# Weight tiles loaded by casting DMAs from GpSimd instead of f32 loads and casts on two engines

## The chip, the cores and the metric

The kernel runs on one core of a Trainium2 chip. The metric is the device time of one execution in microseconds, as the median of several runs. The engines are named as in the profile: PE is TensorE (PEld its weight loads), DVE is VectorE, ACT is ScalarE, POOL is GpSimd, SP is SyncE, which here only issues DMAs. A name with a q behind it (SPq, POOLq) is the queue of that engine.

## The reference, cut to what matters

The program is an attention with two branches, followed by a two-layer dense block.

```python
# batch 8, heads 8, seq 576, head_dim 64; q, k, v float32
q_d, k_d, v_d = means of q, k, v over groups of 4 tokens          # 144 tokens
out_up    = repeat(softmax(q_d @ k_d.T / 8) @ v_d, 4)             # pooled branch
scores    = where(|i - j| < 4, q @ k.T / 8, -1e9)                 # local branch
out_local = softmax(scores) @ v
x = (out_up + out_local) as [4608 tokens, 512]
h = x @ w_in                  # w_in  [512, 2048]
g = h - tanh(h)
out = g @ w_out               # w_out [2048, 512], out [4608, 512] float32
```

## The kernel before, in words

**Attention.** Heads are taken two at a time: 32 head pairs, four to a batch, numbered p = 0 to 31. For each pair, q and k are loaded as f32 into `qkn` (4 buffers), cast and reordered into `qr` (L416), transposed on TensorE (L442) and copied into `qk` (L448). Pairs are pooled over four tokens by two additions (L459, L464). v is loaded in windows of 120 tokens into `vst` (5 buffers) and cast into `vw` (L351, the step `prep_v`). Local scores go to `ps_ts` (L478), exponentials to `E` (L511, L521, L524), a mask is multiplied in (L514, L527), and the products with v go to `ps_ox` (L538, L545). They are normalized into `ln` (L554, L556), transposed back (L566 to L570), and added with the pooled part into `xT` (L597, L599), which holds x transposed in bf16. Pairs 0 to 3 use two sets of PSUM banks in turn; later pairs use one set, since the other becomes the banks `ps_hy` of the dense part. From pair 16 on, the two transposes are DMAs.

**Dense part.** The tokens are taken in 9 blocks of 512. `mm1` (L619) makes 128 of the 2048 hidden columns of a block with four matmuls, ScalarE takes the tanh (L627) and VectorE the difference into `gT` (L630); `mm2` (L646) sums 16 matmuls per 128 tokens, ScalarE copies the result (L657) and SyncE stores it (L660). A block needs all four pairs of its batches. Weights lie in SBUF in bf16, as `w_in_sb` and `w_out_sb`.

**Weights.** `load_w` loads each weight matrix in four tiles f = 0 to 3 of 1 MB (f32), 512 columns of w_in or 512 rows of w_out each. The f32 tile lands in a staging area that is not used otherwise at that time: halves of the two `gT` buffers, or parts of `xT` that belong to batches 4 to 7. Four casts for each tile (L344), each 128 x 512, bring it to bf16 in its place. The DMAs are issued from SyncE (L328, L335, L337): the four tiles of w_in behind the loads of pairs 0 to 3, the tiles of w_out one after another between the loads of pairs 4 to 8 (`ORDER`, `load_next`).

**Order.** The kernel notes every step with an engine, an assumed duration, its reads and writes and a priority (`Program.op`); `choice` names several engines for one step, the casts of weights among them. A planner (`Program.order`) then simulates the engines, with all transfers served one by one, and writes each engine's instructions in the order that it found. The order of each engine is therefore fixed when the program is built. A smaller number is a better priority: dense matmuls have 5000, the steps of pair p have 10 p, the reordering casts 10 p - 12, casts of v 10 p - 12, loads -30. Before the first dense matmul, warm-up matmuls on unused data (L802) are put into the holes of TensorE that the plan shows.

Of the kernel before, what the change touches and what calls it, by code (L numbers as in the profile page):

```python
# [8 lines left out]
FP32 = mybir.dt.float32  # L9
# [6 lines left out]
class Program:  # L16
# [18 lines left out]
    def op(self, eng, ns, fn, reads=(), writes=(), pri=0):  # L35
        i = len(self.ops)
        deps = set()
        for key in reads:
            if key in self.last_write:
                deps.add(self.last_write[key])  # L40
        for key in writes:
            if key in self.last_write:
                deps.add(self.last_write[key])
            deps.update(self.readers.get(key, ()))
        for key in reads:
            self.readers.setdefault(key, set()).add(i)
# [104 lines left out]
def kernel(  # L151
# [9 lines left out]
    nc = tc.nc  # L161
# [3 lines left out]
    NP = H // 2  # L165
# [23 lines left out]
    NQKN, NVST, NVW = 4, 5, 3  # L189
# [25 lines left out]
    gT = fixed("gT", [128, N_FF, 512], BF16, 2)  # L215
# [18 lines left out]
    P = Program()  # L234
    op = P.op
    V, A, T, GP = nc.vector, nc.scalar, nc.tensor, nc.gpsimd
# [45 lines left out]
    def load(ns, fn, keys, cost, pri):  # L282
        op("SP", ns, fn, writes=list(keys) + ["queue", ("q", keys[0])], pri=pri)
        op("DMA", cost, None, reads=[("q", keys[0])], writes=keys, pri=pri)
# [36 lines left out]
                op("DVE", 100, clear, writes=[("vst", s, i)], pri=-99)  # L321
            load(1000, issue, [("vst", s, i)], T_V, -30)

    def load_w(src, dst, name, f, stage, keys):

        def issue():
            if src is moe_w_in:
                nc.sync.dma_start(out=stage.rearrange("p (c f) -> p c f", c=4),  # L328
                                  in_=src[:, 512 * f:512 * f + 512].rearrange(
                                      "(c p) f -> p c f", p=128))  # L330
            else:
                rows = src.rearrange("(f p) n -> p f n", p=128)
                if isinstance(stage, list):
                    for c in range(4):
                        nc.sync.dma_start(out=stage[c], in_=rows[:, 4 * f + c, :])  # L335
                else:
                    nc.sync.dma_start(  # L337
                        out=stage.rearrange("p (c f) -> p c f", c=4),
                        in_=rows[:, 4 * f:4 * f + 4, :])
        load(600, issue, keys, T_W, -30)  # L340
        for c in range(4):
            part = stage[c] if isinstance(stage, list) else stage[:, 512 * c:512 * c + 512]
            to = dst[:, c, 512 * f:512 * f + 512] if src is moe_w_in else dst[:, 4 * f + c, :]
            P.choice([(eng, ns, lambda part=part, to=to, fn=fn: fn(out=to, in_=part))  # L344
                      for eng, ns, fn in CAST], reads=keys, writes=[(name, f, c)],
                     pri=W_PRI + f)


    def prep_v(p):
        s, w, jj = p % NVST, (p // 2) % NVW, p % 2  # L350
        P.choice([(eng, ns, lambda fn=fn: fn(  # L351
            out=vw[w][:, 2 * jj:2 * jj + 2, :, 0:64], in_=vst[s]))
                  for eng, ns, fn in CAST_V[p >= NEARLY]],
                 reads=[("vst", s, 0), ("vst", s, 1)],
                 writes=[("vw", w, jj)], pri=10 * p - 12)
# [327 lines left out]


    M2_FIRST, T_DMA, X_DMA, NEW = 16, 16, 16, 16
    ORDER = "p0p1p2p3"
    T_QK, T_V, T_W, W_PRI, NEARLY = 1150, 900, 2850, -3, NP
    CAST = [("POOL", 700, GP.tensor_copy), ("ACT", 520, A.copy)]
    CAST_V = [[("POOL", 720, GP.tensor_copy), ("ACT", 640, A.copy)],
              [("POOL", 720, GP.tensor_copy)]]  # L690
    any3 = [("DVE", 600, V.tensor_copy), ("ACT", 740, A.copy),
# [9 lines left out]
    for i in range(2):  # L701
        def guards(i=i):
# [3 lines left out]
           writes=[("qk", i, a) for a in range(2)])  # L706
    for i in range(NVW):
        def ones(i=i):
# [3 lines left out]
           writes=[("vd", i), ("vw", i, 0), ("vw", i, 1)])  # L712
        op("POOL", 200, lambda i=i: GP.affine_select(
            out=vd[i][:, 1, :, 64], in_=vd[i][:, 1, :, 64], compare_op=ALU.is_ge,
            fill=0.0, base=-112, pattern=[[0, 4]], channel_multiplier=1),
           writes=[("vd", i)], pri=-96)
    for i in range(2):
        op("DVE", 70, lambda i=i: V.memset(E[i][:, 1728:1840], 0.0),
           writes=[("E", i, 2)], pri=-94)
# [3 lines left out]
    for p in range(NP):  # L723
        if p + 1 < NP:
            load_qk(p + 1)
        load_v(p)
    stages = []
    for g in range(2):
        t = gT[g].rearrange("p f c -> p (f c)").bitcast(FP32)
        for e in range(2):  # L730
            stages.append((t[:, 2048 * e:2048 * e + 2048],
                           [("gT", g, 8 * e + c) for c in range(8)]))
    for e in range(2):
        stages.append(([xT[c][:, 2304 + 1024 * e:3328 + 1024 * e].bitcast(FP32)
                        for c in range(4)],
                       [("x", 4 + 2 * e, c) for c in range(4)]))
    for f in range(4):
        load_w(moe_w_in, w_in_sb, "w_in", f, *stages[f])
    queue = list(ORDER)
    nl = [NP]  # L740

    def load_next():

        while queue and queue[0] != "p":
            f = int(queue.pop(0))
            load_w(moe_w_out, w_out_sb, "w_out", f, *stages[(4, 5, 2, 3)[f]])
        if queue:
            queue.pop(0)
        if nl[0] < NPAIR:
            load_qk(nl[0])  # L750
            load_v(nl[0])
            nl[0] += 1
        if not queue or "p" not in queue:
            while queue:
                f = int(queue.pop(0))
                load_w(moe_w_out, w_out_sb, "w_out", f, *stages[(4, 5, 2, 3)[f]])

    for p in range(2):
        prep_v(p)
    made = 0  # L760
    for i in range(2):
        op("DVE", 70, lambda i=i: V.memset(qkd[i][:, 288:344], 0.0),
           writes=[("qkd", i)], pri=-94)
        op("DVE", 70, lambda i=i: V.memset(vp[i][:, :, :, 64:65], 4.0),
           writes=[("vp", i)], pri=-94)
# [4 lines left out]
    for p in range(NPAIR):  # L770
        if p % 2 == 0 and p < NEW:
            pool_v(p // 2)
        if p + 2 < NPAIR:
            prep_v(p + 2)
        if p == 0:
            next(work[1])
        next(work[p])
        if p + 1 >= NP and p + 1 < NPAIR:
            next(work[p + 1])
        next(work[p], None)  # L780
        if p + 2 < NP:
            next(work[p + 2])
        load_next()
        if NEW <= p + 1 < NPAIR:
            pool_v4(p + 1)
        if NEW <= p + 3 < NPAIR:
            load_v4(p + 3)
        if p % NP == NP - 1:
            b = p // NP
            while made < NBLK and ((made + 1) * 512 - 1) // S <= b:  # L790
                dense(made)
                made += 1
# [41 lines left out]
```

## Time and profile before

| | us |
|---|---|
| median of three runs | 348.71 (348.31 to 348.74) |
| span of the profiled execution | 346.3 |
| the profiled execution's own time | not listed; the span stands for it |
| first dense matmul (L619) starts | 32.06 |
| last instruction of ACT ends | 342.8 |

A row of instructions gives the start in us, the duration in us, the engine, the line, the operation, the tile written and read, the shape, and in brackets the idle time of the engine just before it with what ended it. [...] A group row has the count behind x, then the busy time in all, the mean ns of one, and the idle time before them. An issue row gives the size and the median us from issue to landing.

### The profile page before, as it was taken

The numbers are of one execution on the slowest core, as the hardware profiler recorded it, in microseconds if no ns is written. First come the engines' busy times: TensorE is split into PE (matmuls) and PEld (weight loads), VectorE is DVE, ScalarE is ACT, GpSimd is POOL, SyncE is SP. The second block draws the span as 40 slices with busy tenths as digits, with TensorE's granted clock in tenths as the row PEclk, the third lists the DMA queues.
The fourth block names the chain that finished last, engine by engine and source line by source line (L and its number), as shares of the span: only waits on it lengthen the run. The fifth ranks groups of instructions, "written<-read, shape, count | busy, mean of one in ns | idle before, by whom it ended". The sixth has DMA issues, their size and how long they took to land.

```text
span 346.3 us, 6847 instructions
## 1 busy us (share of the span) xinstructions
PE 328.0 (95%) x2556; PEld 163.5 (47%) x2556; DVE 223.8 (65%) x362; ACT 224.8 (65%) x382; POOL 169.9 (49%) x210
## 2 busy tenths in 40 slices
PE   6787989999999999999999999899999999999995
PEld 2353445555555554445444444444454444444442
DVE  5675788558897968778867677679774443343300
ACT  4585886768978768787878778599753434343411
POOL 6553555575467856887777786958500000000000
PEclk9698999999999999999999999999999999999999
DMA  8999999999999998999999999645231000100021
GB/s 192 234 374 300 277 262 263 217 216 287 212 222 234 252 234 174 226 231 235 261 221 207 260 233 246 157 92 93 57 85 60 31 32 30 61 32 31 30 93 61
DMA packets 103407, 60.74 MB, mean 175 GB/s; under 512 B 77774, under 2 KB 94670, under 8 KB 103374
## 3 DMA queue, kind: packets, MB, share of 16 engines
q1 hardware_dynamic: 103374, 60.30, 78.5%
q8 instruction: 20, 0.33, 0.4%
q14 instruction: 13, 0.11, 0.1%
HBM read 42.46 MB, written 9.44 MB: 150 GB/s over the span
## 4 chain that ended last, share of the span: by engine, by line
PE 69%; DVE 10%; ACT 9%; issue 3%; DMA 3%; POOL 2%; SPq 1%; ACTq 0%; POOLq 0%; DVEq 0%
PE ps_hy_540 L646 8%; PE ps_hy_538 L619 8%; PE ps_hy_539 L619 7%; PE ps_hy_541 L646 7%; PE ps_hy_538 L646 7%; PE ps_hy_539 L646 6%; PE ps_hy_540 L619 6%; PE ps_hy_541 L619 6%; PE ps_ox L538 3%; DVE qr_87 L416 2%; PE ps_ts L478 2%; DMA qkn_73<-in_k_dram 2%; PE ps_ox L545 2%; PE ps_ts L442 2%; PE ps_ox L389 2%
## 5 line engine op out<-in xcount | busy, mean ns | idle before, releaser
L619 PEld LDWEIGHTS <-w_in_sb 128*128 128x128 bf16 x576 | 53.3, 98 | 62.1 <-issue 3.9
L646 PEld LDWEIGHTS <-gT_110 128*128 128x128 bf16 x320 | 30.2, 98 | 34.5
L646 PEld LDWEIGHTS <-gT_111 128*128 128x128 bf16 x256 | 24.0, 98 | 27.4
L459 POOL TENSOR_TENSOR half<-qk_88 128x576 f32<-128x576 bf16 x14 | 16.4, 1169 | 25.3 <-ACT qk_88 L448 11.2
L459 POOL TENSOR_TENSOR half<-qk_89 128x576 f32<-128x576 bf16 x16 | 18.7, 1167 | 19.8 <-ACT qk_89 L448 12.2
L646 PE MATMUL ps_hy_539<-w_out_sb,gT_110 128*128 128x512 bf16 x80 | 20.7, 379 | 0.0
L646 PE MATMUL ps_hy_540<-w_out_sb,gT_110 128*128 128x512 bf16 x80 | 20.4, 379 | 0.0
L646 PE MATMUL ps_hy_538<-w_out_sb,gT_110 128*128 128x512 bf16 x80 | 20.4, 379 | 0.0
L646 PE MATMUL ps_hy_541<-w_out_sb,gT_110 128*128 128x512 bf16 x80 | 20.1, 379 | 0.0
L432 ACT COPY qk_89<-qT_91 128x576 bf16<-128x576 bf16 x16 | 18.7, 1193 | 0.0
L432 ACT COPY qk_88<-qT_90 128x576 bf16<-128x576 bf16 x16 | 18.4, 1188 | 0.0
L511 ACT ACTIVATE E_100<-ps_ts 128x960 bf16<-128x960 f32 x16 | 15.6, 977 | 3.8 <-PE ps_ts L478 3.8
L556 DVE TENSOR_TENSOR ln_106<-ps_ox,r_104 128x896 bf16<-128x896 f32 x16 | 17.4, 1090 | 0.5
L646 PE MATMUL ps_hy_540<-w_out_sb,gT_111 128*128 128x512 bf16 x64 | 16.9, 379 | 0.0
L646 PE MATMUL ps_hy_541<-w_out_sb,gT_111 128*128 128x512 bf16 x64 | 16.8, 379 | 0.0
L646 PE MATMUL ps_hy_539<-w_out_sb,gT_111 128*128 128x512 bf16 x64 | 16.6, 379 | 0.0
L646 PE MATMUL ps_hy_538<-w_out_sb,gT_111 128*128 128x512 bf16 x64 | 16.4, 379 | 0.0
L511 ACT ACTIVATE E_101<-ps_ts 128x960 bf16<-128x960 f32 x14 | 13.6, 973 | 3.8 <-PE ps_ts L478 3.6
L514 DVE TENSOR_TENSOR E_101<-E_101,mask 128x960 bf16<-128x960 bf16 x16 | 13.1, 820 | 3.9 <-ACT E_101 L511 3.7
L556 DVE TENSOR_TENSOR ln_107<-ps_ox,r_105 128x896 bf16<-128x896 f32 x14 | 15.3, 1090 | 0.4
L514 DVE TENSOR_TENSOR E_100<-E_100,mask 128x960 bf16<-128x960 bf16 x16 | 13.6, 847 | 2.8 <-ACT E_100 L511 2.8
L619 PE MATMUL ps_hy_538<-xT_65,w_in_sb 128*128 128x512 bf16 x36 | 13.9, 385 | 1.2 <-DVE xT_68 L599 1.2
(263 smaller groups left out, 890.1 us busy)
## 6 DMA issues: line engine op xcount, KB each, us to landing
out_dram<-y_115 SPq DMA_DIRECT2D x12, 256.0 KB, 2.6
out_dram<-y_116 SPq DMA_DIRECT2D x12, 256.0 KB, 2.3
out_dram<-y_117 SPq DMA_DIRECT2D x12, 256.0 KB, 3.0
qkn_71<-in_q_dram SPq DMA_DIRECT2D x8, 288.0 KB, 7.8
qkn_71<-in_k_dram SPq DMA_DIRECT2D x8, 288.0 KB, 5.8
qkn_72<-in_q_dram SPq DMA_DIRECT2D x8, 288.0 KB, 5.1
qkn_72<-in_k_dram SPq DMA_DIRECT2D x8, 288.0 KB, 5.5
qkn_73<-in_q_dram SPq DMA_DIRECT2D x8, 288.0 KB, 6.6
```

What stands on the lines that cost most here:

```text
L389: T.matmul(pv[:, 0, :], pick[:, t, :], vw[w][:, :, t, 0:64], start=(t == 0), stop=(t == NT - 1))
L416: P.choice([(eng, ns, lambda dst=dst, srt=srt, fn=fn: fn(out=dst, in_=srt)) for eng, ns, fn in REORDER[p >= NEARLY][i]], reads=[("qkn", sn ...
L432: op("ACT", 600, lambda i=i: A.copy(out=full[:, i].rearrange("p (g a) -> p g a", a=A6), in_=qT[s][:, i].rearrange("p a g -> p g a")), read ...
L442: T.transpose(b16[:, G6 * a:G6 * a + G6], qr[s][:, i, a, :], ident[0:G6, 0:G6])
L459: eng.tensor_tensor(out=half, in0=four[:, :, :, 0:2], in1=four[:, :, :, 2:4], op=ALU.add)
L478: T.matmul(sc[:, c:c + NQ[t]], qk[s][rows, k0:k0 + 128], qk[s][rows, QW * t:QW * t + NQ[t]], start=True, stop=True)
L511: op("ACT", 870, lambda: A.activation(out=e1, in_=ps[:, :, 0:480], func=AF.Exp, scale=SCALE), reads=ts, writes=[("E", s, 0)], pri=pri)
L514: op("DVE", 700, lambda: V.tensor_tensor(out=e1, in0=e1, in1=mask[:, 0:480].unsqueeze(1).to_broadcast([128, 2, 480]), op=ALU.mult), reads= ...
L538: T.matmul(po[:, hh, 65 * t:65 * t + 65], E[s][:, c:c + 128], vw[w][:, 2 * jj + hh, t, :], start=True, stop=True)
L556: op("DVE", 1010, lambda: V.tensor_tensor(out=ln[s].rearrange("p n (h d) -> p h n d", d=D), in0=blocks[:, :, :, 0:64], in1=r[s].unsqueeze( ...
L619: T.matmul(ps_hy[slot], w_in_sb[:, dc, fc * 128:(fc + 1) * 128], xT[dc][:, kb * 512:kb * 512 + 512], start=(dc == 0), stop=(dc == N_DC - 1))
L646: T.matmul(ps_hy[slot], gT[g][:, fc, ts * 128:ts * 128 + 128], w_out_sb[:, fc, :], start=(fc == 0), stop=(fc == N_FF - 1))
```

## The change

`load_w` no longer takes a staging area. One DMA for each tile, issued from GpSimd, reads f32 from memory and writes bf16 straight into `w_in_sb` or `w_out_sb`. The 32 casts, the staging areas and the weight DMAs on SyncE go, and with them `CAST`, `W_PRI` and `ORDER`. Each weight DMA has a gate: it is noted as reading `vw` of a certain pair, so it is issued behind the cast of v of that pair (`W_IN_AT`, `W_OUT_AT`: tiles 0 and 1 of w_in behind pair 2, tiles 2 and 3 of w_in and tile 0 of w_out behind pair 3, the other tiles of w_out behind pairs 4, 5 and 6). The planner counts 1.0 us of GpSimd for an issue, with priority -40, and 2.85 us for the transfer, as before.

```diff
-    def load_w(src, dst, name, f, stage, keys):
-
-        def issue():
...
-        load(600, issue, keys, T_W, -30)
-        for c in range(4):
-            part = stage[c] if isinstance(stage, list) else stage[:, 512 * c:512 * c + 512]
-            to = dst[:, c, 512 * f:512 * f + 512] if src is moe_w_in else dst[:, 4 * f + c, :]
-            P.choice([(eng, ns, lambda part=part, to=to, fn=fn: fn(out=to, in_=part))
-                      for eng, ns, fn in CAST], reads=keys, writes=[(name, f, c)],
-                     pri=W_PRI + f)
-
+    def load_w(src, dst, name, f, gate):
+
+        if src is moe_w_in:
+            to = dst[:, :, 512 * f:512 * f + 512]
+            rows = src[:, 512 * f:512 * f + 512].rearrange("(c p) f -> p c f", p=128)
+        else:
+            to = dst[:, 4 * f:4 * f + 4, :]
+            rows = src.rearrange("(f p) n -> p f n", p=128)[:, 4 * f:4 * f + 4, :]
+        op("POOL", 1000, lambda: nc.gpsimd.dma_start(out=to, in_=rows),
+           reads=[gate], writes=[("wq", name, f)], pri=-40)
+        op("DMA", T_W, None, reads=[("wq", name, f)],
+           writes=[(name, f, c) for c in range(4)], pri=-30)
...
-    ORDER = "p0p1p2p3"
-    T_QK, T_V, T_W, W_PRI, NEARLY = 1150, 900, 2850, -3, NP
-    CAST = [("POOL", 700, GP.tensor_copy), ("ACT", 520, A.copy)]
+    W_IN_AT, W_OUT_AT = (2, 2, 3, 3), (3, 4, 5, 6)
+    T_QK, T_V, T_W, NEARLY = 1150, 900, 2850, NP
...
+    def load_ws(p):
+
+        for f in range(4):
+            if W_IN_AT[f] == p:
+                load_w(moe_w_in, w_in_sb, "w_in", f, ("vw", (p // 2) % NVW, p % 2))
+        for f in range(4):
+            if W_OUT_AT[f] == p:
+                load_w(moe_w_out, w_out_sb, "w_out", f, ("vw", (p // 2) % NVW, p % 2))
 
     for p in range(2):
         prep_v(p)
+        load_ws(p)
...
             prep_v(p + 2)
+            load_ws(p + 2)
```

`load_next` keeps the loads of q, k and v, and loses the ones of w_out.

More of the change, by code (lines that the diff above doesn't have):

```diff
@@ L322, in load_v @@
             load(1000, issue, [("vst", s, i)], T_V, -30)
-    def load_w(src, dst, name, f, stage, keys):
-        def issue():
[L327 to L333, printed above, removed]
-                    for c in range(4):
[L335 to L339, printed above, removed]
-        load(600, issue, keys, T_W, -30)
-        for c in range(4):
-            part = stage[c] if isinstance(stage, list) else stage[:, 512 * c:512 * c + 512]
-            to = dst[:, c, 512 * f:512 * f + 512] if src is moe_w_in else dst[:, 4 * f + c, :]
-            P.choice([(eng, ns, lambda part=part, to=to, fn=fn: fn(out=to, in_=part))
-                      for eng, ns, fn in CAST], reads=keys, writes=[(name, f, c)],
-                     pri=W_PRI + f)
+    def load_w(src, dst, name, f, gate):
[9 more added lines that the diff above has]
+           writes=[(name, f, c) for c in range(4)], pri=-30)
     def prep_v(p):
@@ L726 @@
         load_v(p)
[L727 to L739, printed above, removed]
     nl = [NP]
     def load_next():
[L744 to L748, printed above, removed]
         if nl[0] < NPAIR:
@@ L752, in load_next @@
             nl[0] += 1
[L753 to L756, printed above, removed]
+    def load_ws(p):
[5 more added lines that the diff above has]
+                load_w(moe_w_out, w_out_sb, "w_out", f, ("vw", (p // 2) % NVW, p % 2))
     for p in range(2):
         prep_v(p)
+        load_ws(p)
     made = 0
```

## The prediction

> **What bounds the kernel now.** I read the page first, then the busy time by stretches, then the chain of waits ahead of the first dense matmul, then the instructions in order of time on GpSimd and SyncE. The page:
>
> ```profile
> span 346.3 us, 6847 instructions
> PE 328.0 (95%) x2556; PEld 163.5 (47%) x2556; DVE 223.8 (65%) x362; ACT 224.8 (65%) x382; POOL 169.9 (49%) x210
> DMA  8999999999999998999999999645231000100021
> ```
>
> TensorE is busy 95% of the span, but the transfers are busy too, nine tenths or more in nearly every slice until about 220 us. Which of them sets the end in which stretch is seen in the stretches (columns: length, busy time and instructions of each engine, granted clock, share and GB/s of the transfers). The last row of the fence is the same view for the warm-up matmuls (L802) alone.
>
> ```profile
> 0.00:32.00 32.00, 22.63 (x244) 12.44 (x245) 20.62 (x55) 19.50 (x36) 18.15 (x36) 0.89 1.06 272
> 32.00:45.00 13.00, 12.14 (x68) 5.32 (x68) 8.41 (x12) 8.53 (x16) 6.59 (x9) 0.88 1.12 275
> 45.00:76.00 31.00, 30.77 (x316) 17.21 (x314) 21.21 (x34) 23.02 (x44) 18.47 (x24) 1.00 1.18 243
> 76.00:260.00 184.00, 180.37 (x1553) 91.49 (x1552) 146.03 (x221) 142.75 (x234) 126.71 (x143) 1.00 0.97 201
> 0.00:32.00 32.00, 10.28 (x28) 2.86 (x28) 0.89 1.06 272
> ```
>
> From 45 us on TensorE has no room: idle 0.23 us of 31, then 3.6 us of 184. Before 32 us it is idle for 9.4 us and does warm-up work for 10.3 us, and from 32 to 45 us it loses 0.9 us idle and runs at a mean clock of 0.88. So what this change can win, it wins before 45 us, as an earlier or better filled start; after that only lost TensorE time counts. The chain of waits before the first dense matmul:
>
> ```profile
> 24.07 0.60 ACT vd_84 L396
> 25.82 1.10 DVE ln_106 L556
> 29.00 1.10 DVE ln_107 L556
> 31.24 0.77 DVE xT_68 L599
> ```
>
> It is the chain of head pairs 2 and 3; the last piece of xT (31.24 + 0.77) releases the dense part, not a weight.
>
> **What the casts cost, and where.** The eight 1 MB weight tiles are cast in 32 instructions, half on each engine:
>
> ```profile
> L344 POOL CAST w_in_sb<-gT_110 128x512 bf16<-128x512 f32 x4 | 2.4, 617 | 0.8 <-DMA gT_110<-in_moe_w_in_dram 0.8
> L344 ACT CAST w_in_sb<-gT_110 128x512 bf16<-128x512 f32 x4 | 2.3, 627 | 0.0
> 24.55 1.14 ACT L344 CAST w_in_sb<-gT_110 128x512 bf16<-128x512 f32 x2
> 25.59 0.33 ACT L521 ACTIVATE E_101<-ps_ts_123 128x192 bf16<-128x192 f32 x1
> 26.82 0.25 DVE L527 TENSOR_TENSOR E_101<-E_101,mask 128x192 bf16<-128x192 bf16 x1
> 32.06 0.59 PE L619 MATMUL ps_hy_538<-xT_65,w_in_sb 128*128 128x512 bf16 x1 [1.20 <-DVE xT_68 L599]
> ```
>
> 16 x 0.617 + 16 x 0.627 = 19.9 us of engine time go. Most of it lies beside a full TensorE and is worth nothing. One piece is on the chain: the exponential of pair 3 (25.59) comes behind two casts on ScalarE that start at 24.55; vd_84 ends at 24.67, so without them it starts 0.9 us sooner. Then its mask (26.82) no longer has to stand behind ln_106 (25.82 to 26.92), so ln_107 can follow ln_106 directly, at about 27.1 instead of 29.0. Bound of this term: 1.9 us. Its other bound is 0, since pair 4, which arrives sooner (below), puts casts of its own on VectorE with a better priority (28) than pair 3's steps (30). I take the middle, **-1.0 us**.
>
> **What moves on SyncE's queue.** The rows that tell where the weights stand now, and what GpSimd does meanwhile:
>
> ```profile
> 15.14 1.43 SPq L328 DMA_DIRECT2D gT_110<-in_moe_w_in_dram  x2
> 19.00 2.19 SPq L291 DMA_DIRECT2D qkn_71<-in_q_dram  x1
> 22.51 3.94 SPq L316 DMA_DIRECT2D vst_79<-in_v_dram  x2
> 17.31 0.72 POOL L351 CAST vw_81<-vst_77 128x640 bf16<-128x640 f32 x1 [1.66 <-DMA vst_77<-in_v_dram]
> 20.72 1.15 POOL L459 TENSOR_TENSOR half<-qk_89 128x576 f32<-128x576 bf16 x1 [2.68 <-DVE r_105 L554]
> 21.51 0.73 ACT L351 CAST vw_81<-vst_78 128x640 bf16<-128x640 f32 x1
> 31.09 1.17 POOL L344 CAST w_in_sb<-gT_111 128x512 bf16<-128x512 f32 x2 [2.42 <-DMA gT_111<-in_moe_w_in_dram]
> 33.38 0.82 POOL L416 CAST qr_86<-qkn_71 96x768 bf16<-96x768 f32 x1 [1.12 <-DMA qkn_71<-in_k_dram]
> gT_110<-in_moe_w_in_dram SPq DMA_DIRECT2D x2, 1024.0 KB, 8.9
> qkn_71<-in_q_dram SPq DMA_DIRECT2D x8, 288.0 KB, 7.8
> vst_75<-in_v_dram SPq DMA_DIRECT2D x13, 160.0 KB, 6.1
> ```
>
> Now four weight tiles go out from 15.14 us, and pair 4's q and k stand behind them, issued from 19.00, used at 33.38. Afterwards SyncE issues no weight (14 instructions less: 4, 8 and 2), and pair 4's loads go out at about 15.1; with the 7.8 us to landing of such a load they arrive near 23 us instead of 33. The weights come on a second queue, behind a gate: two tiles after the v cast of pair 2 (17.31 + 0.72 = 18.0 us), three after that of pair 3 (21.51 + 0.73 = 22.2 us), then one each after pairs 4, 5 and 6.
>
> What this is worth: TensorE starts the dense part slowed.
>
> ```profile
> 32.44 0.63 PE L619 MATMUL ps_hy_538<-xT_66,w_in_sb 128*128 128x512 bf16 x1
> 32.86 0.63 PE L619 MATMUL ps_hy_538<-xT_67,w_in_sb 128*128 128x512 bf16 x1
> 35.29 0.38 PE L619 MATMUL ps_hy_540<-xT_65,w_in_sb 128*128 128x512 bf16 x1
> 35.50 0.38 PE L619 MATMUL ps_hy_540<-xT_66,w_in_sb 128*128 128x512 bf16 x1
> ```
>
> The pitch is 0.42 us at first and 0.21 us later; the first eight matmuls take 35.29 - 32.06 = 3.2 us instead of 1.7. With pair 4's transposes and scores at hand, TensorE has work in the hole before the dense part. Bounds: 0 if the hole stays, 1.5 + 0.9 (the idle time from 32 to 45 us) = 2.4 if all goes. I take **-1.5 us**, the slow start alone, because the idle 0.9 us is spread over waits that have nothing to do with loads.
>
> **Are the weights in time?** When they are needed is seen in how fast the first dense block used them (view of L619 by stretches):
>
> ```profile
> 32.00:36.00 4.00, 3.94 (x12) 1.43 (x11) 0.61 1.11 315
> 36.00:40.00 4.00, 3.31 (x15) 1.14 (x14) 1.00 1.20 210
> 40.00:45.00 5.00, 3.86 (x19) 1.68 (x18) 1.00 1.08 294
> ```
>
> A tile serves 16 matmuls, so tile 2 is first used at about 37 us, tile 3 at 41.5, tile 4 at 46, though the last one was there near 32 (31.09 + 1.17). The new queue shares the same transfer engines with SyncE's, which has the loads of pairs 4 to 7 queued. At half of the 275 GB/s a tile of 1.05 MB takes 7.6 us, at two thirds 5.7. The first issue ends near 19, so the four land at 27, 34, 42 and 50 by the half, at 25, 30, 36 and 42 by two thirds. The packets of a weight row (512 elements of f32) are larger than those of v (64 elements), so I expect more than half. By that nothing is late by more than a microsecond or two, which pair 4's and 5's matmuls cover; I cost it at 0. Without that cover the fourth tile costs 50 - 46 = 4 us.
>
> **What GpSimd pays.** Eight issues come, each first in priority (-40), and everything behind one waits on GpSimd in order: pair 3's pooling (L459, 20.72), later the k cast (33.38) and v cast of pairs 4 to 6; ScalarE's gate for pair 3 is a new wait of the GpSimd queue. No row shows an issue from GpSimd. The nearest rows are SyncE's: 0.7 us each for the weights (1.43 for two), up to 3.94 for two v loads (2.0 each) when its queue is full, and the single largest here is 2.19. The cast that an issue replaces took 0.617, four of them on GpSimd's share of two tiles. Bounds: 0.7 and 2.2 us. I take 1 us, near the unhindered one, as the new queue starts empty. Two such issues from 18.03 end at 20.0; GpSimd was idle 2.68 us until 20.72, so they are covered up to 1.34 us each. The three after 22.2 replace eight casts that stood there until 32.3 (8 x 0.617 = 4.9 us), so they are covered too, up to about 3 us each ((32.3 - 22.2) / 3), unless pair 3's second pooling step stands behind them. Cost: 0.
>
> A row that speaks of GpSimd and VectorE in each other's way is the q cast; columns are shortest, median and longest ns:
>
> ```profile
> L416 DVE CAST qr_87<-qkn_72 x8: 543/786/2391, 6.5 to 214.3; 96x768 bf16<-96x768 f32 x8
> ```
>
> The same cast takes 0.54 to 2.4 us. [...]
>
> **The sum.** -1.0 - 1.5 + 0 + 0 = -2.5 us, against the profiled span of 346.3 us: 343.8. The listing gives no time of its own for that execution; the median of the runs is 348.71, 2.4 us above the span, for what lies around it, and I carry that over: **346.2 us**. With one of the two terms at its end the likeliest case runs from 345.3 (-3.4) to 347.7 (-1.0). What a measurement here can tell from no change is about 0.2%, 0.7 us.
>
> **Rivals.**
> - Full gain: both terms at their best ends, -1.9 - 2.4 = -4.3, so 344.4 us. For it: 9.4 us idle and 10.3 us warm-up before 32 us. Against it: VectorE is busy 20.6 us of those 32 and its chain sets the start.
> - No difference, 348.7 us: pair 4 arriving early takes back what pair 3 gains, and from 45 us on TensorE is full anyway.
> - GpSimd held by its issues, slower: with 2.2 us each, the two after 18.03 end at 22.4, so pair 3's pooling starts 1.7 us late, the next three hold GpSimd until about 29, and if pair 3's second pooling step stands behind them the start of the dense part moves by 3 x 2.2 = 6.6 us less what is saved: 348.7 + 1.7 + 6.6 - 2.5 = 354.5 us. It decides from 1.34 us an issue. For it: the spread of the q cast, the full transfer queues. Against: the planner may give pair 3's pooling to VectorE, and the slack after 22.2.
> - Two queues where the planner counts one, slower: the written order is fixed by a plan in which transfers are served one by one. If weights take half of the 275 GB/s, the 896 KB of a pair (2 x 288 + 2 x 160) take 6.7 us instead of 3.3, and TensorE stands in its order before a pair's transposes while dense work is ready behind them. Pairs 5 and 6 late by 3.3 each, less 2.5: 348.7 + 4.1 = 352.8 us. For it: transfers full until 220 us. Against: without 4 MB ahead of them these pairs have a lead of 10 us.
>
> **Numbers.** Forecast 0.40, full gain 0.10, no difference 0.10, GpSimd held 0.22, two queues 0.18. So faster 0.50, same 0.10, slower 0.40. The range reaches from 343.8 (the full gain less what a measurement can tell) to 355.0 (just past GpSimd held) and leaves out about 0.05 below and 0.12 above, for bounds that are themselves guessed; the likeliest case alone is 345.3 to 347.7.
>
> **What would show it.** Right: no L344; pair 4's k cast before 28 us; the first L619 near 31 us at a pitch of 0.21; GpSimd issues near 1 us. Wrong: a GpSimd issue over 1.34 us or L459 of pair 3 later than 21 us; L619 waiting on a weight; TensorE idle over 1 us between 32 and 76 us, waiting on L416; a stretch after 76 us with more idle time than 3.6 us.

## The result and the profile after

| | before | after |
|---|---|---|
| median of nine runs, us | 348.71 (346.72 to 350.26) | 352.85 (350.85 to 357.32) |
| ratio | | 1.0119, interval 1.0078 to 1.0159 |
| profiled execution: time, span | time not listed, span 346.3 | 351.22, span 349.5 |
| first dense matmul starts | 32.06 | 37.65 |

The changed kernel is slower by 1.2%, where the forecast was 0.7% faster. Ratios, here and below, use only executions within 1.5% of their kernel's fastest (seven of the nine after), and the profiled execution of x_spread lies outside. Lines have moved: L607 is `mm1` (L619 before), L634 `mm2`, L332 the new weight DMA, L339 the cast of v, L377 the pooling matmul of v, L404 the cast of q and k, L430 the transposes, L587 the last piece of xT. The page after, at its head and in the DMA slices:

```profile
span 349.5 us, 6784 instructions
PE 327.2 (94%) x2553; PEld 164.9 (47%) x2553; DVE 226.9 (65%) x371; ACT 218.4 (62%) x366; POOL 161.0 (46%) x193
DMA  8999999999987899999999999735332100010021
```

The span is 3.2 us longer. The stretches say where (same columns as before):

```profile
0.00:32.00 32.00, 24.05 (x260) 14.09 (x261) 23.58 (x58) 17.98 (x31) 20.92 (x36) 0.95 1.11 215
32.00:45.00 13.00, 9.18 (x89) 5.66 (x89) 5.94 (x9) 6.48 (x12) 6.58 (x7) 0.87 1.20 217
45.00:76.00 31.00, 29.86 (x268) 15.67 (x267) 21.01 (x34) 19.68 (x38) 13.38 (x17) 1.00 1.17 229
76.00:260.00 184.00, 178.34 (x1529) 90.55 (x1527) 146.98 (x227) 141.69 (x231) 117.48 (x130) 1.00 0.95 193
```

TensorE's idle time went from 0.86 to 3.82 us between 32 and 45 us, from 0.23 to 1.14 between 45 and 76, and from 3.63 to 5.66 between 76 and 260. Most of the first is one hole, from 30.74 to 35.03 us. In the chain of waits (start, length, what) and in the order of time it looks like this:

```profile
18.50 11.52 DMA vst<-in_v_dram
30.06 4.18 issue
34.26 0.73 POOL vw L339
35.03 1.22 PE ps_ox L377 x5
```

```profile
18.50 3.07 SPq L316 DMA_DIRECT2D vst<-in_v_dram  x2
25.44 1.66 POOL L404 CAST qr<-qkn 96x768 bf16<-96x768 f32 x2
30.59 0.76 DVE L587 TENSOR_TENSOR xT<-ps_ox,od 128x576 bf16<-128x576 bf16 x1 [0.49 <-ACT od L585]
34.26 0.72 POOL L339 CAST vw<-vst 128x640 bf16<-128x640 f32 x1 [7.16 <-DMA vst<-in_v_dram]
35.03 1.22 PE L377 MATMUL ps_ox<-vw,pick 128*128 128x256 bf16 x5 [4.29 <-POOL vw L339]
37.65 0.74 PE L607 MATMUL ps_hy<-xT,w_in_sb 128*128 128x512 bf16 x2
```

The two v loads of pair 5 are issued from 18.5 us on and used at 34.26: the first lands at 30.02, the second only at 34.2. GpSimd waits 7.16 us for them, TensorE 4.29 us for GpSimd. The dense part could have begun when xT ended, at 31.35 us (the first tile of w_in had landed at 28.7), but in the written order the pooling of pair 5's v, and after it pair 5's transposes, stand ahead of the first dense matmul. That second load took 14.2 us from issue to landing, as the issue row of that stretch (19.2 to 22 us) says, where the median of all v loads is 7.4 (issue rows, KB each, median us):

```profile
vst<-in_v_dram SPq DMA_DIRECT2D x2, 160.0 KB, 14.2
vst<-in_v_dram SPq DMA_DIRECT2D x62, 160.0 KB, 7.4
```

No wait of TensorE in the trace is on a weight, and the weights' own issues are cheap (shortest, median, longest ns):

```profile
L332 POOL DMA_DIRECT2D w_in_sb<-in_moe_w_in_dram x4: 746/764/903, 17.8 to 22.6; - x4
L332 POOL DMA_DIRECT2D w_out_sb<-in_moe_w_out_dram x4: 745/762/780, 23.3 to 47.2; - x4
```

Why v is late shows in the transfer queues between 24 and 32 us (packets, MB, share of 16 engines; q0 is GpSimd's queue, q1 SyncE's; q0's MB are those written, in bf16):

```profile
q0 software_dynamic: 1244, 1.24, 91.5%
q1 hardware_dynamic: 1174, 0.32, 29.0%
```

The queues move nearly the same number of packets. A weight packet writes 1 KB (2 KB read); one on SyncE's queue has 0.27 KB on average, since nearly all of them here are v's rows of 256 bytes. So SyncE's queue, with loads of pairs 5 and 6 on it, gets 0.32 MB in 8 us, 40 GB/s. (The two shares come to 120.5%: the times of packets overlap.)

### The profile page after: what moved, and what is told of

Same layout as the page of the kernel before. It is cut to its first block, busy times and chain, and to the rows that moved or that the text cites. A ratio compares the mean times of both kernels' runs of the same rounds, so it can differ in the third digit from the quotient of the medians.

```text
span 349.5 us, 6784 instructions
## 1 busy us (share of the span) xinstructions
PE 327.2 (94%) x2553; PEld 164.9 (47%) x2553; DVE 226.9 (65%) x371; ACT 218.4 (62%) x366; POOL 161.0 (46%) x193
## 4 chain that ended last, share of the span: by engine, by line
PE 70%; DMA 9%; DVE 7%; ACT 6%; issue 4%; SPq 3%; POOL 1%; ACTq 0%; POOLq 0%; DVEq 0%
PE ps_hy L607 29%; PE ps_hy L634 29%; DMA vst<-in_v_dram 7%; ACT qk L420 3%; PE ps_ts L466 2%; PE ps_ox L526 2%; DVE gT L618 2%; PE ps_ts L430 2%; PE ps_ox L533 1%; SPq L291 1%; DVE xT L576 1%; DMA qkn<-in_q_dram 1%; ACT u L615 1%; PE ps_ox L377 1%; PE ps_ox L558 1%
## 5 line engine op out<-in xcount | busy, mean ns | idle before, releaser
L607 PE MATMUL ps_hy<-xT,w_in_sb 128*128 128x512 bf16 x576 | 146.3, 380 | 3.6 <-DVE gT L618 3.4
L634 PE MATMUL ps_hy<-w_out_sb,gT 128*128 128x512 bf16 x576 | 142.8, 380 | 0.0
L618 DVE TENSOR_TENSOR gT<-ps_hy,u 128x512 bf16<-128x512 f32 x144 | 97.1, 685 | 65.3 <-ACT u L615 64.3
L615 ACT ACTIVATE u<-ps_hy 128x512 f32<-128x512 f32 x144 | 84.3, 599 | 73.1 <-PE ps_hy L607 72.5
L634 PEld LDWEIGHTS <-gT 128*128 128x128 bf16 x576 | 54.2, 98 | 62.3
L607 PEld LDWEIGHTS <-w_in_sb 128*128 128x128 bf16 x576 | 52.8, 98 | 62.3 <-issue 4.4
L447 POOL TENSOR_TENSOR half<-qk 128x576 f32<-128x576 bf16 x30 | 35.9, 1196 | 46.3 <-ACT qk L436 26.9
L420 ACT COPY qk<-qT 128x576 bf16<-128x576 bf16 x32 | 36.8, 1185 | 0.0
L544 DVE TENSOR_TENSOR ln<-ps_ox,r 128x896 bf16<-128x896 f32 x32 | 34.8, 1088 | 0.9
L499 ACT ACTIVATE E<-ps_ts 128x960 bf16<-128x960 f32 x32 | 31.1, 971 | 5.5 <-PE ps_ts L466 5.5
L404 POOL CAST qr<-qkn 96x768 bf16<-96x768 f32 x31 | 28.5, 921 | 8.3 <-PE ps_ts L430 5.8
L339 POOL CAST vw<-vst 128x640 bf16<-128x640 f32 x31 | 23.3, 753 | 15.9 <-DMA vst<-in_v_dram 15.9
L404 DVE CAST qr<-qkn 96x768 bf16<-96x768 f32 x33 | 23.2, 705 | 7.1 <-DMA qkn<-in_q_dram 5.9
L526 PEld LDWEIGHTS <-E 128*128 128x128 bf16 x320 | 16.4, 98 | 10.0 <-DVE E L515 3.5
```

The lines of the kernel that those rows point to most:

```text
L339: P.choice([(eng, ns, lambda fn=fn: fn(out=vw[w][:, 2 * jj:2 * jj + 2, :, 0:64], in_=vst[s])) for eng, ns, fn in CAST_V[p >= NEARLY]], rea ...
L404: P.choice([(eng, ns, lambda dst=dst, srt=srt, fn=fn: fn(out=dst, in_=srt)) for eng, ns, fn in REORDER[p >= NEARLY][i]], reads=[("qkn", sn ...
L420: op("ACT", 600, lambda i=i: A.copy(out=full[:, i].rearrange("p (g a) -> p g a", a=A6), in_=qT[s][:, i].rearrange("p a g -> p g a")), read ...
L447: eng.tensor_tensor(out=half, in0=four[:, :, :, 0:2], in1=four[:, :, :, 2:4], op=ALU.add)
L499: op("ACT", 870, lambda: A.activation(out=e1, in_=ps[:, :, 0:480], func=AF.Exp, scale=SCALE), reads=ts, writes=[("E", s, 0)], pri=pri)
L526: T.matmul(po[:, hh, 65 * t:65 * t + 65], E[s][:, c:c + 128], vw[w][:, 2 * jj + hh, t, :], start=True, stop=True)
```

## The experiments

Two theories were set against each other. **Theory 1:** loads shared with the weights land later than the plan assumed, and the written order then holds TensorE. **Theory 2:** the new order is worse by itself. Where a third reading was at stake, the expectation says it. Ratios are against the kernel before on the same chip.

**x_plan: the plan told the measured load times.** DMAs and gates are the changed kernel's; in the plan the weights get a server of their own, `WQ`. Dots in an edit stand for lines that are not shown.

```diff
+    QK_AT = {(6, 0): 2050, (6, 1): 3000, (7, 0): 2000, (7, 1): 2400}
+    V_AT = {5: 4500, 6: 3500, 7: 2500}
+    W_AT = {"w_in": (8100, 3300, 4000, 3900), "w_out": (3400, 3500, 4400, 3600)}
...
-        op("DMA", T_W, None, reads=[("wq", name, f)],
+        op("WQ", W_AT[name][f], None, reads=[("wq", name, f)],
```

> The changed kernel with the same DMAs, gates and steps; only the planner is told other load times, those that the profile of the changed kernel shows (weight tiles landing from 28.7 us on, one every 3 to 4 us, on a queue of their own; v of pair 5 at 34 us, the loads of pairs 6 and 7 at 36 to 56 us), so only the written order of the engines differs. Theory 1 (the second queue delays the loads of pairs 5 to 7 against the plan, and TensorE stands in its written order before the pooling of pair 5's v): the idle 4.3 us ahead of the v pooling of pairs 4 and 5 goes to under 0.5 us, the first dense matmul starts at 31 to 32 us instead of 37.7, and the time falls by 3 to 5 us to 347.5 to 350 us. Theory 2 (the loss is in the casting DMAs themselves or in GpSimd's issues): no change, 351 to 354 us.

Measured: 349.92 us, ratio 1.0057 (1.0012 to 1.0102). In the order of time, in a stretch, and among TensorE's waits (us in total, times, longest):

```profile
31.87 1.02 PE L607 MATMUL ps_hy<-xT,w_in_sb 128*128 128x512 bf16 x4 [0.76 <-DVE xT L587]
```

```profile
55.00:60.00 5.00, 2.96 (x15) 0.95 (x12) 0.00 (x0) 0.99 (x2) 3.24 (x4) 0.82 1.11 233
```

```profile
PE ps_hy L634 <- DMA w_out_sb<-in_moe_w_out_dram: 2.0, 1, 2.0
```

The first dense matmul is back at 31.87, and the first hole is gone. A new one stands at 55 us: TensorE waits 2.0 us for the last tile of w_out, whose DMA is noted behind the first dense block, so that the planner does not see the wait. Half of the loss came back (1.0119 to 1.0057), though the two intervals overlap; the rows and the time came out as theory 1 had them.

**x_stage: f32 loads from GpSimd, casts kept.** The staging areas and the 32 casts of the kernel before, the gates of the changed one, except that the last tile of w_out goes out behind pair 5.

```diff
-                nc.sync.dma_start(out=stage.rearrange("p (c f) -> p c f", c=4),
+                nc.gpsimd.dma_start(out=stage.rearrange("p (c f) -> p c f", c=4),
...
-        load(600, issue, keys, T_W, -30)
+        op("POOL", 1000, issue, reads=[gate],
+           writes=list(keys) + [("wq", name, f)], pri=-40)
+        op("DMA", T_W, None, reads=[("wq", name, f)], writes=keys, pri=-30)
```

> The weights are issued from GpSimd behind the same gates (the last w_out tile behind pair 5 instead of 6), but as f32 into the staging areas, and the 32 casts are kept: the second queue without the cast on the way. Theory 1 (it is the second queue): v of pair 5 is cast after 32 us again and TensorE idles 3 us or more before it; 352 to 358 us, as the casts come on top. Theory 2 (it is the cast on the way that makes the transfers slow): v of pair 5 is cast before 29 us as planned, no such hole, 347 to 350 us.

Measured: 372.74 us, ratio 1.0711 (1.0650 to 1.0771). Order of time, and the waits of TensorE:

```profile
28.92 0.54 POOL L335 DMA_DIRECT2D xT<-in_moe_w_out_dram  x1 [2.94 <-DMA gT<-in_moe_w_in_dram]
41.85 0.72 POOL L352 CAST vw<-vst 128x640 bf16<-128x640 f32 x1 [1.44 <-DMA vst<-in_v_dram]
```

```profile
PE ps_ts L443 <- POOL qr L417: 10.9, 1, 10.9
```

The time is over 14 us above either theory's number, and it tells nothing between them: GpSimd, which now has fourteen weight DMAs, stood 2.94 us before the ninth until a tile of w_in had landed, 2.43 to 2.82 us before each of the next three likewise, and TensorE waited 10.9 us for a q or k cast behind them. The loads do tell something. Pair 5's v is late here too: its loads were issued from 18.18 us on, the first took 16.4 us to land, and the trace puts the wait before its cast at 41.85 down to a load of v. The queues between 24 and 32 us, with f32 written:

```profile
q0 software_dynamic: 681, 2.66, 92.1%
q1 hardware_dynamic: 679, 0.19, 11.4%
```

Without a cast on the way the packet counts are equal as well, the packets of weights are larger, and SyncE's queue gets even less. So v is late without the cast on the way, and theory 2 of this run falls by its loads.

**x_fewcast: the kernel before with 8 of its 32 casts.** Loads and staging unchanged; the dense matmuls read tile 2 of w_in and tile 0 of w_out throughout.

```diff
+        if (name, f) not in (("w_in", 2), ("w_out", 0)):
+            return
         for c in range(4):
             part = stage[c] if isinstance(stage, list) else stage[:, 512 * c:512 * c + 512]
...
```

> The kernel before with 24 of its 32 weight casts left out (those of one tile of w_in and one of w_out are kept, and all dense matmuls read these two tiles); all loads stay as they are, on SyncE's queue. It prices the removed casts alone. By the first term of the prediction (0 to 1.9 us, taken at 1.0) the first dense matmul starts at 30.1 to 32.0 us and the time is 346.5 to 348 us. If the casts lie off the path: 32.0 us and 348.5 to 349 us.

Measured: 347.38 us, ratio 0.9966 (0.9930 to 1.0002). In the order of time:

```profile
30.04 3.61 PE L621 MATMUL ps_hy<-xT,w_in_sb 128*128 128x512 bf16 x16 [1.20 <-DVE xT L601]
```

Without 24 of the casts the first dense matmul starts 2.0 us earlier, near the prediction's upper bound of 1.9. The time falls by 1.2 us, but the interval reaches from 2.4 us less to 0.1 us more, so a gain from the casts themselves is likely and not certain.

**x_vrows: v in rows of 1280 bytes.** The changed kernel; each v load reads 128 rows of 320 values instead of 640 rows of 64, so other tokens, the same bytes.

```diff
-                    nc.sync.dma_start(out=t[:, i], in_=win(-4, 128, 5))
+                    nc.sync.dma_start(
+                        out=t[:, i].rearrange("p a d -> p (a d)"),
+                        in_=bass.AP(tensor=base.tensor, offset=base.offset,
+                                    ap=[[287, 128], [1, 320]]))
```

> The changed kernel, but v is loaded in rows of 1280 B, one for each partition, instead of five of 256 B (other tokens of v, the same number of bytes). If the two queues take turns by packet, small rows lose against the 2 KB rows of the weights: v of pair 5 lands within 9 us of its issue instead of 15, its cast starts before 28 us, the hole on TensorE before it falls under 1 us, and weight tiles land more slowly than one in 3.8 us. If the weights win whatever the size of the rows: v of pair 5 is cast after 32 us as before.

Measured: 345.59 us in one run, which is not compared: nearly all v loads of the kernel have a fifth of the packets. Order of time, then the queues between 24 and 32 us:

```profile
27.53 0.72 POOL L342 CAST vw<-vst 128x640 bf16<-128x640 f32 x1 [0.23 <-DMA vst<-in_v_dram]
```

```profile
q0 software_dynamic: 902, 0.90, 66.5%
q1 hardware_dynamic: 900, 1.17, 49.0%
```

With all the weights in flight pair 5's v is cast at 27.53. Again the queues move equal numbers of packets, 902 and 900; only now 900 packets are 1.17 MB instead of 0.32. The queues had nearly equal shares of the packets in both windows, 1244 to 1174 and 902 to 900; what makes them equal is not shown. What follows for the bytes is measured too: the queue with the small rows got 0.32 of 1.56 MB, and with its longer rows 1.17 of 2.07 MB.

**x_fewload: two of eight weight DMAs issued.** Order of every engine as in the changed kernel.

```diff
-        op("POOL", 1000, lambda: nc.gpsimd.dma_start(out=to, in_=rows),
+        op("POOL", 1000, (lambda: nc.gpsimd.dma_start(out=to, in_=rows)) if f == 0 else None,
...
```

> The changed kernel with the order of every engine kept, but only two of the eight weight DMAs issued (tile 0 of w_in and tile 0 of w_out); the dense matmuls read these two tiles throughout, so the product is not the reference's. It takes away the transfers of 6 MB and nothing else. Theory 1 (the loads of v run beside the weights on the transfer engines and land later than the plan assumed; the fixed order then holds TensorE): the v cast of pair 5 starts near 27 us instead of 34.26, the first dense matmul near 32 instead of 37.65, and the time falls by 3 to 5 us from 352.85, to 348-350. Theory 2 (the new order itself is worse, whatever the transfers do): the hole and the time stay, 351-354. Lower than 347 would say that weights cost more than the hole.

Measured: 348.66 us, ratio 0.9982 (0.9935 to 1.0028). In the order of time:

```profile
32.80 0.72 POOL L339 CAST vw<-vst 128x640 bf16<-128x640 f32 x1 [4.33 <-DMA vst<-in_v_dram]
33.58 1.22 PE L377 MATMUL ps_ox<-vw,pick 128*128 128x256 bf16 x5 [3.22 <-POOL vw L339]
```

The time came out as theory 1 had it, the cast did not: 32.80, not 27. The two tiles that were kept are 1.05 MB of the 1.51 MB that the changed kernel writes between 17 and 33 us, so too little was taken away there. The hole shrank by only 1.1 us; TensorE's idle time between 45 and 260 us fell by more, from 6.8 to 4.4 us. So the time is no proof of what the hole costs, and the run was repeated with less.

**x_sixteenth: 128 columns of w_in and 128 rows of w_out.** Same order again.

```diff
-        op("POOL", 1000, lambda: nc.gpsimd.dma_start(out=to, in_=rows),
+        if src is moe_w_in:
+            to, rows = to[:, :, 0:128], rows[:, :, 0:128]
+        else:
+            to, rows = to[:, 0:1, :], rows[:, 0:1, :]
+        op("POOL", 1000, (lambda: nc.gpsimd.dma_start(out=to, in_=rows)) if f == 0 else None,
...
```

> The changed kernel with the order of every engine kept, but of the weights only 128 columns of w_in and 128 rows of w_out loaded, a sixteenth; the dense matmuls read these throughout. The run with two of eight tiles took away too little where it counts: its two tiles are nearly all that lands before 33 us in the changed kernel too (2.5 tiles by 34 us). Theory 1 (transfers shared with the weights make v of pair 5 late): its cast starts at 26.5 to 28 us (34.26 with all the weights, 32.80 with two tiles), the idle time before the pooling matmul (4.29, then 3.22) goes, the first dense matmul starts at 30.5 to 33, and the time is 346 to 348.5. Theory 2 (the load queue of SyncE is late by itself, weights or not): the cast stays after 30 us and the time at 348 to 350.

Measured: 344.42 us, ratio 0.9912 (0.9879 to 0.9945). Order of time, then the stretches, then the queues between 24 and 32 us:

```profile
30.17 0.72 POOL L343 CAST vw<-vst 128x640 bf16<-128x640 f32 x1 [1.14 <-DMA vst<-in_v_dram]
33.58 0.60 PE L611 MATMUL ps_hy<-xT,w_in_sb 128*128 128x512 bf16 x2
```

```profile
32.00:45.00 13.00, 12.04 (x135) 6.81 (x134) 9.68 (x17) 11.26 (x20) 6.50 (x9) 1.00 1.22 206
45.00:76.00 31.00, 31.00 (x284) 16.80 (x282) 20.38 (x34) 18.96 (x36) 11.92 (x15) 1.00 0.80 167
76.00:260.00 184.00, 179.03 (x1508) 90.27 (x1508) 145.55 (x224) 140.71 (x230) 116.73 (x129) 1.00 0.90 186
```

```profile
q1 hardware_dynamic: 3225, 1.65, 109.1%
q0 software_dynamic: 209, 0.15, 11.8%
```

This is the run that settles it. The same order takes 0.9% less than the kernel before when fifteen sixteenths of the weights are not moved, and 1.2% more when they are. The difference of the ratios, 2.07%, is 7.2 us. (Six of the eight issues, 0.76 us each on GpSimd, go too; x_plan2 below keeps all eight and has no hole.) By the profiles, TensorE's idle time over the span is 22.3 us in the changed kernel and 16.1 here; the hole at pair 5 is 4.3 of these 6.2 us. SyncE's queue gets 1.65 MB in the 8 us where it got 0.32. Theory 1 missed three of its numbers: the cast at 30.17 is later than 26.5 to 28, the first dense matmul at 33.58 later than 30.5 to 33, and the time, 1.6 us under the low end of its range of 346 to 348.5, is better. The loads are 3 us behind the plan even so, but no wait of TensorE from 28 to 76 us is on v, and the clock is full from 32 to 260 us. Theory 2 falls by the time; what it says of SyncE's queue being late by itself is right for 3 us that cost nothing here.

**x_tw: one assumed time, 3.80 us for a weight.**

```diff
-    T_QK, T_V, T_W, NEARLY = 1150, 900, 2850, NP
+    T_QK, T_V, T_W, NEARLY = 1150, 900, 3800, NP
```

> The changed kernel with only one assumed time changed: 3.80 us for a weight transfer, the measured distance between two landings, instead of 2.85; the planner still serves all transfers one by one and pair 4's and 5's loads ahead of the weights. If the size of the assumed time was the fault, the hole goes and the time falls to 349-350. If the sharing is what the planner misses, v of pair 5 is still planned for 27 us and cast after 33, the hole of 4 us stays, and the time is 352 to 355.

Measured: 353.25 us, ratio 1.0169 (1.0110 to 1.0229). In the order of time:

```profile
36.42 1.23 PE L377 MATMUL ps_ox<-vw,pick 128*128 128x256 bf16 x5 [6.56 <-POOL vw L339]
```

The hole stays and grows to 6.56 us, so a larger assumed time alone is no cure. What is left as the fault is that the plan serves pair 4's and 5's loads in full before the weights, where the queue rows show both served at once; x_plan and x_plan2, whose plans know the landing times, bear it out.

**x_spread: later gates.**

```diff
-    W_IN_AT, W_OUT_AT = (2, 2, 3, 3), (3, 4, 5, 6)
+    W_IN_AT, W_OUT_AT = (2, 3, 4, 5), (5, 5, 5, 5)
```

> The changed kernel with the planner as it was and only the gates moved: w_in tile by tile behind pairs 2, 3, 4 and 5, w_out behind pair 5. Theory 1: one tile in flight instead of two beside pair 5's v, so its cast moves from 34.26 to 29-32 and the hole before the pooling matmul falls from 4.3 to under 2.5 us; but the planner's single transfer server still misjudges the weights, so tiles 1 to 3 of w_in are planned when they are not needed: 348.5 to 351.5. Theory 2 (the gates do not matter): 352 to 354, hole of 4 us.

Measured: 357.15 us, ratio 1.0260 (1.0185 to 1.0335); the profiled execution took 360.59. In the order of time:

```profile
31.22 0.71 POOL L339 CAST vw<-vst 128x640 bf16<-128x640 f32 x1
32.65 2.98 POOL L332 DMA_DIRECT2D w_out_sb<-in_moe_w_out_dram  x4
41.89 0.72 POOL L339 CAST vw<-vst 128x640 bf16<-128x640 f32 x1 [5.42 <-DMA vst<-in_v_dram]
44.89 0.42 PE L482 MATMUL ps_ts<-qkd 64*128 64x144 bf16 x4 [4.54 <-POOL qkd L452]
```

Pair 5's cast is at 31.22, as theory 1 had it, and that hole is gone. But five tiles now go out from 31.9 us together, and the next v, pair 6's, is cast at 41.89; GpSimd waits for it with a pooling step behind it, and TensorE waits 4.54 us for that. A second hole, of 3.95 us before 57.68, waits for xT. The expected time (348.5 to 351.5) was missed by 6 us, and both theories' numbers fall. That the late loads are the cause here too fits these rows and is not shown by a run of its own.

**x_plan2: x_plan, and the last tile of w_out behind pair 5.**

```diff
...
-    W_IN_AT, W_OUT_AT = (2, 2, 3, 3), (3, 4, 5, 6)
+    W_IN_AT, W_OUT_AT = (2, 2, 3, 3), (3, 4, 5, 5)
```

> The changed kernel with the planner told the measured load times (as in the run before) and the gate of the last tile of w_out moved from pair 6 to pair 5, so that the tile stands ahead of the first dense block in the program and the planner knows that mm2 waits for it. Theory 1: no hole at 34 us and none at 55 to 60 (TensorE waited 2.0 us for that tile there and ran at a clock of 0.82 afterwards); 347 to 348.5 us, that is level with the kernel before or 1 us better. Theory 2 (any order that starts dense work so early runs into another wait): 349 to 351, with a hole of 2 us or more somewhere from 45 to 76 us.

Measured: 346.60 us, ratio 0.9980 (0.9944 to 1.0016). By stretches:

```profile
32.00:45.00 13.00, 12.24 (x113) 6.65 (x110) 10.16 (x17) 10.34 (x19) 6.11 (x8) 1.00 1.20 218
45.00:76.00 31.00, 30.97 (x305) 16.82 (x302) 20.12 (x32) 20.22 (x37) 16.57 (x19) 1.00 1.19 239
76.00:260.00 184.00, 177.11 (x1503) 89.56 (x1503) 146.97 (x223) 139.93 (x228) 118.75 (x133) 1.00 0.97 192
```

Both holes are gone although every weight is moved, only the last tile one pair earlier than in the changed kernel, and the clock is full. The whole loss is recovered, and the kernel is level with the one before; a gain of 0.2% can't be told from none. Against x_sixteenth (0.9912), 0.7% is still missing, so the gain that the prediction had hoped for does not show in any kernel that moves all its weights on the second queue.

**x_plan3: the same table, gates (2, 2, 3, 4) and (4, 5, 5, 5).**

```diff
...
-    W_IN_AT, W_OUT_AT = (2, 2, 3, 3), (3, 4, 5, 6)
+    W_IN_AT, W_OUT_AT = (2, 2, 3, 4), (4, 5, 5, 5)
```

> The changed kernel with the planner told the measured load times and the weight tiles issued later: tiles 0 and 1 of w_in behind pair 2, tile 2 behind pair 3, tile 3 and tile 0 of w_out behind pair 4, the rest of w_out behind pair 5. Theory 1: fewer weights in flight beside pair 5's loads, so its v cast is at hand by 31 to 34 us and no wait on TensorE over 1 us from 32 to 76 us: 346.5 to 348, a chance to be below the kernel before. Theory 2 (the gain of an early start is given back later, since the ratio of dense work to attention work left is what it is): as with all weights early, 347.5 to 348.5, level with before.

Measured: 348.38 us, ratio 1.0029 (0.9992 to 1.0066). No wait of TensorE between 32 and 76 us is over 0.5 us. Level with before, by theory 2's number; later gates bring nothing more.

**x_poolcast: the kernel before, casts of w_in on GpSimd alone.**

```diff
-                      for eng, ns, fn in CAST], reads=keys, writes=[(name, f, c)],
+                      for eng, ns, fn in (CAST[:1] if src is moe_w_in else CAST)], reads=keys, writes=[(name, f, c)],
```

> The kernel before with one edit: the sixteen casts of w_in all go to GpSimd (those of w_out still have the choice), so no weight cast stands on ScalarE before pair 3's exponential. If the first term of the prediction is right (the casts on ScalarE hold pair 3's chain by up to 1.9 us), the first dense matmul moves from 32.06 to 30-31 and the time falls by 0.5 to 1.5 us, to 347-348. If not (the later casts on GpSimd hold the dense part or pair 4), the first dense matmul waits on w_in instead of xT and the time is 348.5 to 351.

Measured: 351.21 us, ratio 1.0106 (1.0052 to 1.0159). Order of time, then a stretch:

```profile
30.92 5.34 PE L619 MATMUL ps_hy<-xT,w_in_sb 128*128 128x512 bf16 x24 [1.21 <-DVE xT L599]
57.45 1.66 ACT L344 CAST w_out_sb<-gT 128x512 bf16<-128x512 f32 x3 [1.89 <-DMA gT<-in_moe_w_out_dram]
```

```profile
45.00:76.00 31.00, 27.13 (x272) 14.79 (x270) 16.19 (x27) 19.84 (x38) 16.54 (x21) 1.00 1.06 230
```

The dense part starts 1.1 us earlier, as the first term has it, and the time still rises by 1.1%: TensorE is idle 3.87 us between 45 and 76 us. One thing seen there is ScalarE waiting 1.89 us before 57.45 for a late f32 tile of w_out, with the exponential of a pair behind it. TensorE's own waits on casts of w_out come to only 0.6 us from 28 to 76 us, so what the late tile costs is not shown. An early start alone was no gain.

**x_ctrl: a control.** The kernel before with one assumed time changed.

```diff
-    T_QK, T_V, T_W, W_PRI, NEARLY = 1150, 900, 2850, -3, NP
+    T_QK, T_V, T_W, W_PRI, NEARLY = 1150, 900, 3000, -3, NP
```

> A control: the kernel before with only one assumed time of the planner changed, 3.00 us instead of 2.85 for a weight transfer. Instructions and transfers are the same, only the order that the planner writes differs. It shows how much a re-drawn order moves the time without any change of the work. If differences of 1 us between these kernels mean something, it stays within 0.7 us of 348.4; if the draw of the order alone makes 1 to 3 us, it can land anywhere from 347 to 352.

Measured: 348.22 us, ratio 1.0019 (0.9988 to 1.0049). A re-drawn order that keeps all work moved the time by at most half a per cent here, in one draw. The 1.2% of the change and the 2.1% between it and x_sixteenth are larger than that. The run shows one thing more. Its dense part starts without the slow pitch:

```profile
32.44 2.75 PE L619 MATMUL ps_hy<-xT,w_in_sb 128*128 128x512 bf16 x12 [1.20 <-DVE xT L599]
```

Twelve matmuls take 2.75 us, and the granted clock is 1.00 from 32 to 45 us, although pair 4's k is cast as late as before (34.25 us). The time is the same.

## Why the prediction was wrong

The direction was wrong, and the step that failed is **"Are the weights in time?"**, costed at 0. Its own question was answered rightly: the weights won more than half of the bytes (1.24 of the 1.56 MB that were written between 24 and 32 us, with half of the packets), and no matmul waited for a weight. What it left out is the other side of the share: the weights in flight leave SyncE's queue 0.32 MB in 8 us. Part of the cover that it named, pair 5's matmuls, was the very thing that became late.

The price stood in the prediction itself, in the rival **two queues where the planner counts one**, at 352.8 us; 352.85 was measured. The mechanism is that rival's, but an agreement to 0.05 us is luck. It let weights take half of the bytes where they took four fifths, had pairs 5 and 6 late by 3.3 us each (6.6 in all, less 2.5), and had TensorE stand before a pair's transposes. In the trace one hole of 4.29 us, before the pooling of pair 5's v, is the largest piece, and the price by the runs is 7.2 us. Its chance of 0.18 was too small: the argument against it, a lead of 10 us, counted the issue times (pair 5's v was issued from 18.5 us on) and not the landings, up to 14.2 us later.

The other steps:
- **Casts off pair 3's chain, -1.0 us.** The mechanism is right: in x_fewcast the two normalizations of the chain follow each other at 25.71 and 26.99 us, and xT ends 2.0 us earlier. The size fits (-1.2 us), but with an interval of -2.4 to +0.1. In the changed kernel itself xT ends only 0.66 us earlier (31.35 for 32.01): there the normalizations start at 26.61 and 28.35, with a q or k cast on VectorE (27.61) between them, which is the prediction's reason for its lower bound.
- **Pair 4's loads earlier, -1.5 us.** Pair 4's k and another cast stand at 25.44, for 33.38 before, as was said. That this takes the slow start away is not shown. The clock from 32 to 45 us is 0.87 after and 1.00 in x_sixteenth, but it is 1.00 in x_ctrl too, where pair 4 is as late as before and the time is the same. Nor was the slow start a fixed cost: over the 72 executions of the kernel before that the ratios of the experiments use, the mean clock ran from 0.980 to 1.000, and 0.999 or more in 13 of them, against 0.984 in the profiled one. The term was sized on one execution. Both terms together gave -2.5; x_sixteenth's ratio says -3.1 (-4.2 to -1.9), but it moves hardly any weights, and x_plan2, which moves them all, says -0.7 (-2.0 to +0.6).
- **GpSimd's issues, 0.** Right: 0.745 to 0.903 us, with VectorE at work beside them, under the 1.34 us where it would matter. The prediction's row of the q cast tells of VectorE's casts and not of an issue. In the trace of before the 11 of these casts with GpSimd idle take 0.54 to 0.56 us, and the 14 that take longer than 0.65 us all have GpSimd at work beside them (at 168.50 us 3.27 us), though others beside it take 0.55 (at 101.96); what makes the long ones long is not shown. Beside an issue such a cast was not held: at 23.14 us of the changed kernel it took 0.57 us.
- **Later idle time.** The 2.0 us more between 76 and 260 us, a sign of being wrong that came true, are not explained. The largest sum of waits there is 3.4 us of `mm1` for gT, but x_plan2, at the time of before, has 6.89 us idle in that stretch with only 0.5 us of this wait. It is left open.

## What to carry to other kernels

When loads move to a second queue, cost what the first queue loses, packet against packet (here SyncE's queue moved 0.32 MB in 8 us, and 1.65 in x_sixteenth, without most of the weights), and ask which instruction in the written order waits for the load that becomes late. A plan that serves transfers one by one misjudged two queues here: give it measured landing times, and let it see every wait (x_plan and x_plan2 took back 0.6% and 1.4%). An earlier start need not be a gain: x_poolcast started 1.1 us earlier and was slower by 1.1%. And before a slow clock is costed as a loss, see whether other executions of the same kernel have it (mean clock 0.980 to 1.000 here).

## What was not expected of the hardware

- Two queues with work shared the engines by packets, whatever their size, in all these windows: 1244 to 1174 with rows of 2 KB against 256 bytes, 902 to 900 when most of the small rows had 1280 bytes, 681 to 679 with weight packets of 3.9 KB (x_stage). In the changed kernel the four stretches of 4 us from 32 to 48 us have 489 and 491, 595 and 594, 633 and 629, 485 and 489.
- A DMA that casts on the way cost the transfer engines no more here than one that doesn't, though the packets of the two differ in size too. The queue rows of the changed kernel and of x_stage (packets, MB written, share of 16 engines over the span) give 7.1% x 16 x 349.5 / 8 = 49.6 us of engine time for a tile with the cast and 6.8% x 16 x 370.3 / 8 = 50.4 without it, at half the bytes written:

```profile
q0 software_dynamic: 4224, 4.19, 7.1%
```

```profile
q0 software_dynamic: 2272, 8.39, 6.8%
```

- GpSimd can be held by its own weight DMAs: in x_stage GpSimd stood 2.94 us before the ninth issue, for a tile of w_in to land, and 2.43 to 2.82 us before each of the next three; the eight of the changed kernel never waited. Whether the chip or the program makes it wait there was not tried.
